# Twelve VectorE additions of the first MoE layer made into ScalarE copies with accumulating DMAs

## The chip, the cores and the metric

The kernel runs on one core of a Trainium2 chip. The metric is the device time of one execution in microseconds, lower is better. A run gives several executions; the median is compared.

## The reference, cut to what matters

The kernel fuses three layers: attention with a tanh cap, a first MoE layer (w1, w2) and a second one (w3, w4) with a softmax-like gate and a layer norm. The change lies in the second product of the first MoE layer.

```python
def _moe_ref(x, w_in, w_out):       # x 1792 x 768, w_in 768 x 2048, w_out 2048 x 768
    h = x @ w_in
    g = h - np.tanh(h)
    return (g @ w_out).astype(np.float32)
...
x = attention(q, k, v, cap)         # (1792, 768)
x = _moe_ref(x, moe_w_in, moe_w_out)
return _moe2_ref(x, moe2_w_in, moe2_w_out, moe2_g_ln)
```

## The kernel before, in words

The work is done in two halves of 896 tokens (`hb` 0 and 1), each in three stages: attention, `moe1`, `moe2`. Every matrix product is made of three matmuls on high and low parts (`wh`, `wl` of a weight, `xh`, `xl` or `gh`, `gl` of an activation).

**Weights.** They come as pairs of 32-bit words. In the first half a unit of weights (512 KB) is loaded into a staging tile `st` (L104, three buffers, SyncE's DMA queue, called SP below), three VectorE instructions put the words together in `f` (L109, L110, L111; three buffers), ScalarE writes the high part (L117) and VectorE the low part (L118). SP then saves the result to HBM (L134, `d<-w`), where the second half reads it, so that only the first half converts. In what follows, a conversion is one such L109, L110, L111 and L118. The conversion runs many units ahead of the matmuls, through a ring of 14 weight tiles.

**moe1.** The hidden dimension is cut into four chunks (`NCHUNK`). `up(c)` makes four blocks `hp` of 128 hidden rows by 896 tokens in PSUM (pool "a", two buffers; L416, L418), and `nonlinear` (L442 to L460) turns each into `gh` and `gl`: ScalarE reads `hp` twice (L444 into `u`, L446 into `t`), VectorE twice (L450 and L453), and after L453 the PSUM buffer is free. Tiles `u` have two buffers. `down(c)` makes six output blocks `op` (L472, L474; pool "b", two buffers), 24 matmuls each, and adds each to its accumulator `acc[d]` in SBUF: for chunk 0 ScalarE copies (L479), for later chunks VectorE adds in two instructions of 448 columns (L481); the last chunk also splits the sum into `yh` and `yl` (L483, L484). TensorE runs up(1), down(0), up(2), down(1), up(3), down(2), down(3).

**Order of the work.** In `moe1` the order of each engine's queue is set by the framework's scheduler, which goes by its own estimates; once the program is built each engine runs its list strictly in order. GpSimd's queue (POOL) carries in this stage only the DMAs that wait for the next attention.

Of the kernel before, what the change touches and what calls it, by code (L numbers as in the profile page):

```python
# [9 lines left out]
F32 = mybir.dt.float32  # L10
# [4 lines left out]
ALU = mybir.AluOpType  # L15
# [14 lines left out]
def fused_kernel(ctx, tc, qk_in, v, cap, w1, w2, w3, w4, gln, out):  # L30
    nc = tc.nc
    B, H, S, D = 4, 12, 448, 64
    DM = H * D
    P = 128
# [14 lines left out]
    NCHUNK = w2.shape[0] // NK  # L49
# [11 lines left out]
    @contextmanager  # L61
    def banks(name, *tags):
        with ExitStack() as st:
            for tag, n in tags:
                psum[tag] = st.enter_context(tc.tile_pool(name=name + tag, bufs=n, space=PSUM, reuse_waits="tile"))
            yield

    def pst(name, tag="b"):
        return psum[tag].tile([P, 2, 512], F32, tag=tag, name=name)
# [130 lines left out]
    def load_w1(c, half):  # L200
        ts = []
        for i in range(NK // 2):
            ts += cols(unit(f"1_{c}_{half}_{i}", w1u[(c * 2 + half) * (NK // 2) + i], 2), 2)
        return ts

    def load_w2(c, d):
        return cols(unit(f"2_{c}_{d}", w2u[c * NK + d], CH // P), CH // P)
# [193 lines left out]
        while pending:  # L401
            keep()

    def moe1(mp, xh, xl, yh, yl):
        acc = [mp.tile([P, HT], F32, tag=f"acc{d}", name=f"acc{d}", bufs=1) for d in range(NK)]
        gs = {}
        place.update(pool=(mp, WX1), at=-1)

        def up_mms(hp, wt, m, k0, k1, gg=(0, 1)):
            ms = slice(m * P, (m + 1) * P)  # L410
            for kk in range(k0, k1):
                wh, wl = wt[kk]
                xs = [(xh[kk][:, g * S:(g + 1) * S], xl[kk][:, g * S:(g + 1) * S]) for g in range(2)]
                for i in range(2):
                    for g in gg:
                        nc.tensor.matmul(hp[:, g, :S], wh[:, ms], xs[g][i], start=(kk == 0 and i == 0), stop=False)  # L416
                for g in gg:
                    nc.tensor.matmul(hp[:, g, :S], wl[:, ms], xs[g][0], start=False, stop=(kk == NK - 1))  # L418

        def first():  # L420

            gs[0] = []
            wts = [load_w1(0, 0), load_w1(0, 1)]
            hps = [pst("hp", "ab"[half]) for half in range(2) for _ in range(2)]
            for g, k0, k1 in ((0, 0, NK), (1, 0, 3), (1, 3, 4), (1, 4, 5), (1, 5, 6)):
                for m in range(3):
                    up_mms(hps[m], wts[m // 2], m % 2, k0, k1, (g,))
                    if k1 == NK and g == 1:
                        nonlinear(0, hps[m])
            up_mms(hps[3], wts[1], 1, 0, NK)  # L430
            nonlinear(0, hps[3])

        def up(c, half):
            gs.setdefault(c, [])
            wt = load_w1(c, half)
            for m in range(2):
                hp = pst("hp", "a")
                up_mms(hp, wt, m, 0, NK)
                nonlinear(c, hp)

        def nonlinear(c, hp):
            h = hp[:, :, :S]  # L442
            u = mp.tile([P, 2, S], F32, tag="u", name="u")
            nc.scalar.activation(u, h, AF.Square)  # L444
            t = mp.tile([P, 2, S], F32, tag="t", name="t")
            nc.scalar.activation(t, h, AF.Tanh)  # L446
            mk = mp.tile([P, 2, S], U8, tag="mk", name="mk")
            nc.scalar.activation(mk, t, AF.Square, scale=TS)
            gf = mp.tile([P, 2, S], F32, tag="gf", name="gf")
            nc.vector.scalar_tensor_tensor(gf, u, C2, h, ALU.mult, ALU.mult)  # L450
            w = mp.tile([P, 2, S], F32, tag="w", name="w", bufs=1)
            nc.scalar.activation(w, u, AF.Square, bias=gat)
            nc.vector.tensor_tensor(t, h, t, ALU.subtract)  # L453
            nc.vector.scalar_tensor_tensor(gf, w, GB, gf, ALU.add, ALU.mult)
            nc.vector.copy_predicated(gf, mk, t)
            gh = mp.tile([P, 2, S], F32R, tag="gh", name="gh", bufs=6)
            gl = mp.tile([P, 2, S], F32R, tag="gl", name="gl", bufs=6)
            nc.scalar.copy(gh, gf)  # L458
            nc.vector.tensor_tensor(gl, gf, gh.bitcast(F32), ALU.subtract)
            gs[c].append((gh, gl))  # L460

        def down(c):
            for d in range(NK):
                wt = load_w2(c, d)
                op = pst("op")
                nm = CH // P
                for m in range(nm):
                    gg = gs[c][m]
                    wh, wl = wt[m]
                    for i in range(2):  # L470
                        for g in range(2):
                            nc.tensor.matmul(op[:, g, :S], wh, gg[i][:, g], start=(m == 0 and i == 0), stop=False)  # L472
                    for g in range(2):
                        nc.tensor.matmul(op[:, g, :S], wl, gg[0][:, g], start=False, stop=(m == nm - 1))  # L474
                for g in range(2):
                    cs = slice(g * S, (g + 1) * S)
                    a = acc[d][:, cs]
                    if c == 0:
                        nc.scalar.copy(a, op[:, g, :S])  # L479
                    else:  # L480
                        nc.vector.tensor_tensor(a, op[:, g, :S], a, ALU.add)  # L481
                    if c == NCHUNK - 1:
                        nc.scalar.copy(yh[d][:, cs], a)  # L483
                        nc.vector.tensor_tensor(yl[d][:, cs], a, yh[d][:, cs].bitcast(F32), ALU.subtract)  # L484

        first()
        for c in range(NCHUNK):
            if c + 1 < NCHUNK:
                up(c + 1, 0)
                up(c + 1, 1)  # L490
            down(c)
# [136 lines left out]
    @contextmanager  # L628
    def pools(name, *groups):
        with ExitStack() as st:  # L630
            yield Region([(g, st.enter_context(tc.tile_pool(name=f"{name}{i}", bufs=2, reuse_waits="tile")))
                          for i, g in enumerate(groups)])

    def xtiles():
        return ([xp.tile([P, HT], F32R, tag="xh", name="xh") for _ in range(NK)],
                [xp.tile([P, HT], F32R, tag="xl", name="xl") for _ in range(NK)])

    rest = None
    for hb in range(2):
        xh, xl = xtiles()  # L640
        with pools(f"a{hb}", ("t",), ("kqh", "kql"), ("ou",), ("rb", "rs", "su"), None) as ap, banks(f"pa{hb}", ("s", 1), ("o", 2)):
            with tc.manual_schedule(engines=ORD):
                attention(ap, hb, xh, xl, rest)
        yh, yl = xtiles()
        if hb == 0:
            nc.sync.dma_start(glt, gln.rearrange("(c p) -> p c", p=P))
        with pools(f"m{hb}", ("gh", "gl"), ("wx",), ("acc",), None) as mp, banks(f"pm{hb}", ("a", 2), ("b", 2)):
            moe1(mp, xh, xl, yh, yl)
        with pools(f"n{hb}", ("h2g",), ("wx",), ("lh0", "ll0"), None, ("e",), ("lh1", "ll1")) as mp, banks(f"pn{hb}", ("a", 2), ("b", 2)):
            rest = moe2(mp, hb, yh, yl)  # L650

# [62 lines left out]
```

## Time and profile before

| | |
|---|---|
| three runs | 931.48, 932.25, 938.44 us; median 932.25 |
| profiled execution | 931.82 us, of which the profile's span is 930.0 |
| mean granted TensorE clock | 0.991 |
| instructions | 12258 |

The profile holds for each engine every instruction with start and duration, and for a wait what ended it. Times in it are microseconds from the start of the span. The span is one execution, so a sum made from it is compared with 931.82 first and then set beside the median.

### The profile page before, as it was taken

The page shows a single profiled execution, that of the slowest core. Times are in us where ns is not written, and L with a number is a line of the kernel's source. Part 1 is how long each engine was busy: PE and PEld are TensorE (multiplying, and loading weights), DVE is VectorE, ACT ScalarE, POOL GpSimd, SP SyncE. Part 2 cuts the span into 40 slices and gives each one's busy share as a digit, 9 for nine tenths or more (in the row PEclk, how much of TensorE's full clock was granted, in tenths as well). Part 3 has the DMA queues.
Part 4 walks back from the last instruction along what each step waited for, and adds up shares of the span by engine and source line. Part 5 has one row for each costly group of instructions (what it writes and reads, how often), then busy time and mean ns, then how long its engine had stood idle before and what let it go on. Part 6 is the DMA issues. An engine that isn't in the chain of part 4 may idle for free.

```text
span 930.0 us, 12258 instructions
## 1 busy us (share of the span) xinstructions
PE 909.5 (98%) x4864; PEld 736.2 (79%) x4864; DVE 583.8 (63%) x918; ACT 418.1 (45%) x459; POOL 46.8 (5%) x88
## 2 busy tenths in 40 slices
PE   6999998999999999999999999999999999999998
PEld 4444487999989998888874446899999999888887
DVE  5677589999989994688423443793363644305851
ACT  6999328546335222352258882573340511212321
POOL 2211000000000000001022110000000000000000
PEclk9999989999999999999999999999999999999999
DMA  7564383398685875531154641524333232221311
GB/s 246 160 210 131 112 334 128 104 329 290 215 270 194 276 272 205 173 146 78 53 201 167 204 137 38 171 79 133 105 113 113 86 124 87 91 83 53 134 48 51
DMA packets 49500, 142.92 MB, mean 154 GB/s; under 512 B 13540, under 2 KB 16612, under 8 KB 49444
## 3 DMA queue, kind: packets, MB, share of 16 engines
q1 hardware_dynamic: 42260, 112.95, 35.4%
q0 software_dynamic: 7040, 29.20, 9.3%
q8 instruction: 38, 0.62, 0.3%
q14 instruction: 18, 0.15, 0.1%
q10 hardware_dynamic: 144, 0.00, 0.0%
HBM read 98.64 MB, written 43.33 MB: 153 GB/s over the span
## 4 chain that ended last, share of the span: by engine, by line
PE 74%; DVE 12%; DMA 9%; issue 2%; ACT 2%; SPq 0%; DVEq 0%; ACTq 0%
PE op L472 13%; PE hp L416 9%; PE op L474 6%; PE o L302 6%; PE s L270 5%; PE hp L418 4%; PE hp L223 4%; PE hp L224 4%; PE hp L225 4%; PE so L319 3%; DMA rs<-su 2%; PE oab L572 2%; PE oab L576 2%; PE oab L573 2%; DMA rb<-rd 2%
## 5 line engine op out<-in xcount | busy, mean ns | idle before, releaser
L416 PE MATMUL hp<-xh,w 128*128 128x448 f32 x384 | 118.2, 374 | 9.2 <-DVE t L453 4.8
L416 PE MATMUL hp<-xl,w 128*128 128x448 f32 x384 | 117.3, 372 | 0.4 <-DVE xl L361 0.4
L418 PE MATMUL hp<-xh,w 128*128 128x448 f32 x384 | 116.0, 369 | 0.0
L474 PE MATMUL op<-gh,w 128*128 128x448 f32 x336 | 95.7, 365 | 0.0
L472 PE MATMUL op<-gl,w 128*128 128x448 f32 x336 | 95.4, 365 | 0.0
L472 PE MATMUL op<-gh,w 128*128 128x448 f32 x336 | 95.4, 365 | 0.0
L416 PEld LDWEIGHTS hp<-xh,w 128*128 128x128 f32 x384 | 73.4, 192 | 18.8 <-issue 7.0
L416 PEld LDWEIGHTS hp<-xl,w 128*128 128x128 f32 x384 | 73.8, 192 | 8.8 <-issue 1.4
L418 PEld LDWEIGHTS hp<-xh,w 128*128 128x128 f32 x384 | 73.1, 190 | 5.9
L302 PE MATMUL o<-t,vf 128*64 128x448 f32 x384 | 77.5, 545 | 0.0
L294 ACT ACTIVATE t<-t,shift,capt 128x3136 f32<-128x3136 f32 (+2 forms) x26 | 72.7, 2806 | 0.7
L481 DVE TENSOR_TENSOR acc<-op,acc 128x448 f32<-128x448 f32 x72 | 41.8, 617 | 44.6 <-PE op L474 44.5
L472 PEld LDWEIGHTS op<-gh,w 128*128 128x128 f32 x336 | 63.1, 188 | 5.0
L472 PEld LDWEIGHTS op<-gl,w 128*128 128x128 f32 x336 | 63.1, 188 | 5.0
L474 PEld LDWEIGHTS op<-gh,w 128*128 128x128 f32 x336 | 63.1, 188 | 5.0
L223 PE MATMUL hp<-w,xh 128*128 128x512 f32 x168 | 65.5, 390 | 0.0
L225 PE MATMUL hp<-w,xl 128*128 128x512 f32 x168 | 65.4, 389 | 0.0
L224 PE MATMUL hp<-w,xh 128*128 128x512 f32 x168 | 65.4, 389 | 0.0
L458 ACT CAST gh<-gf 128x896 fp32r<-128x896 f32 x32 | 30.2, 944 | 72.5 <-PE op L474 47.4
L444 ACT ACTIVATE u<-hp 128x896 f32<-128x896 f32 x32 | 29.5, 920 | 71.2 <-PE hp L418 71.0
L117 ACT CAST w<-f 128x512 fp32r<-128x512 f32 x44 | 27.3, 622 | 71.9 <-DVE f L111 52.2
L302 PEld LDWEIGHTS o<-t,vf 128*64 128x64 f32 x384 | 25.4, 136 | 40.8 <-issue 40.2
(146 smaller groups left out, 1681.0 us busy)
## 6 DMA issues: line engine op xcount, KB each, us to landing
d<-w SPq DMA_DIRECT2D x69, 512.0 KB
w<-d SPq DMA_DIRECT2D x56, 512.0 KB
st<-in_moe_w_out_dram SPq DMA_DIRECT2D x35, 512.0 KB
st<-in_moe_w_in_dram SPq DMA_DIRECT2D x25, 512.0 KB
kq<-in_qk_dram POOLq DMA_DIRECT2D x21, 480.0 KB, 5.0
w<-d POOLq DMA_DIRECT2D x13, 512.0 KB, 6.0
st<-in_moe_w_in_dram POOLq DMA_DIRECT2D x11, 512.0 KB, 6.0
vf<-in_v_dram POOLq DMA_DIRECT2D x22, 256.0 KB, 5.0
```

The lines of the kernel that those rows point to most:

```text
L223: nc.tensor.matmul(ps, sh, mh, start=first, stop=False)
L224: nc.tensor.matmul(ps, sh, ml, start=False, stop=False)
L225: nc.tensor.matmul(ps, sl_, mh, start=False, stop=last)
L270: nc.tensor.matmul(s[:, 2 * r + hh, :S], st[rows, cs], mv[rows, KW:], start=first, stop=last)
L294: nc.scalar.activation(t[:, sl], t[:, sl], AF.Exp, bias=shift, scale=capt)
L302: nc.tensor.matmul(o[cs, :S], vf[:, r, cs], t[:, 6 if r == 3 else 2 * r + hh], start=(r == 0), stop=(r == 3))
L416: nc.tensor.matmul(hp[:, g, :S], wh[:, ms], xs[g][i], start=(kk == 0 and i == 0), stop=False)
L418: nc.tensor.matmul(hp[:, g, :S], wl[:, ms], xs[g][0], start=False, stop=(kk == NK - 1))
L458: nc.scalar.copy(gh, gf)
L472: nc.tensor.matmul(op[:, g, :S], wh, gg[i][:, g], start=(m == 0 and i == 0), stop=False)
L474: nc.tensor.matmul(op[:, g, :S], wl, gg[0][:, g], start=False, stop=(m == nm - 1))
L481: nc.vector.tensor_tensor(a, op[:, g, :S], a, ALU.add)
```

## The change

In the first half only (`hb == 0`), for the two middle chunks (c = 1 and 2), the finished block `op` is copied out whole by ScalarE (896 columns, from PSUM) into a tile `part`, and a DMA issued by GpSimd adds `part` to `acc[d]` (`accum_op=ALU.add`). `part` takes its buffers from the tag `u`, the two buffers that the nonlinearity's squares use. The two VectorE additions for that block are left out. The second half is unchanged.

```diff
-    def moe1(mp, xh, xl, yh, yl):
+    def moe1(mp, hb, xh, xl, yh, yl):
...
+                if hb == 0 and 0 < c < NCHUNK - 1:
+                    part = mp.tile([P, 2, S], F32, tag="u", name="part")
+                    nc.scalar.copy(part, op[:, :, :S])
+                    nc.gpsimd.dma_start(acc[d], part.rearrange("p g s -> p (g s)"), accum_op=ALU.add)
+                    continue
                 for g in range(2):
...
-            moe1(mp, xh, xl, yh, yl)
+            moe1(mp, hb, xh, xl, yh, yl)
```

The scheduler makes new lists for VectorE and ScalarE from it. VectorE's list before, at the end of down(1)'s stretch and up to the first nonlinearity of up(3) (L450 on `hp_2329`); `f` and `st` numbers name single conversions:

```order
L109 TENSOR_SCALAR f_2851<-st_2849 128x512
L118 TENSOR_TENSOR wx_2768<-f_2771,wx_2768 128x512
L118 TENSOR_TENSOR w_2806<-f_2809,w_2806 128x512
L110 SCALAR_TENSOR_TENSOR f_2851<-st_2849,f_2851 128x512
L111 SCALAR_TENSOR_TENSOR f_2851<-st_2849,f_2851 128x512
L109 TENSOR_SCALAR f_2893<-st_2891 128x512
L110 SCALAR_TENSOR_TENSOR f_2893<-st_2891,f_2893 128x512
L111 SCALAR_TENSOR_TENSOR f_2893<-st_2891,f_2893 128x512
L450 SCALAR_TENSOR_TENSOR gf_2372<-u_2366,hp_2329 128x896
L109 TENSOR_SCALAR f_2935<-st_2933 128x512
L454 SCALAR_TENSOR_TENSOR gf_2372<-w_2374,gf_2372 128x896
L453 TENSOR_TENSOR t_2368<-hp_2329,t_2368 128x896
```

From the last VectorE instruction that is the same in both lists (L454 of up(2)'s fourth block) to this L450 the list holds 10 conversions (their L109, L110 and L111), 10 L118, 12 additions L481, one L455 and two L459. The same place in the changed program (the block is called `hp_2335` there):

```order
L110 SCALAR_TENSOR_TENSOR f_2905<-st_2903,f_2905 128x512
L118 TENSOR_TENSOR w_2860<-f_2863,w_2860 128x512
L111 SCALAR_TENSOR_TENSOR f_2905<-st_2903,f_2905 128x512
L109 TENSOR_SCALAR f_2947<-st_2945 128x512
L110 SCALAR_TENSOR_TENSOR f_2947<-st_2945,f_2947 128x512
L111 SCALAR_TENSOR_TENSOR f_2947<-st_2945,f_2947 128x512
L109 TENSOR_SCALAR f_2989<-st_2987 128x512
L110 SCALAR_TENSOR_TENSOR f_2989<-st_2987,f_2989 128x512
L111 SCALAR_TENSOR_TENSOR f_2989<-st_2987,f_2989 128x512
L450 SCALAR_TENSOR_TENSOR gf_2378<-u_2372,hp_2335 128x896
L454 SCALAR_TENSOR_TENSOR gf_2378<-w_2380,gf_2378 128x896
L453 TENSOR_TENSOR t_2374<-hp_2335,t_2374 128x896
```

The same stretch now holds 12 conversions, 11 L118, no addition, one L455 and two L459: two more conversions stand ahead of L450. ScalarE's list before, over the same stretch, from the casts of down(1) to `u` of up(3)'s first block:

```order
L117 CAST w_2692<-f_2695 128x512
L458 CAST gh_2010<-gf_2003 128x896
L458 CAST gh_2064<-gf_2057 128x896
L117 CAST w_2730<-f_2733 128x512
L117 CAST wx_2768<-f_2771 128x512
L117 CAST w_2806<-f_2809 128x512
L444 ACTIVATE u_2366<-hp_2329 128x896
```

And in the changed program, from the copy of down(1)'s fourth block on (the first three copies stand ahead, with casts between them):

```order
L477 COPY part_2221<-op_2196 128x896
L117 CAST w_2740<-f_2743 128x512
L117 CAST wx_2779<-f_2782 128x512
L477 COPY part_2260<-op_2235 128x896
L458 CAST gh_2010<-gf_2003 128x896
L117 CAST w_2818<-f_2821 128x512
L458 CAST gh_2064<-gf_2057 128x896
L477 COPY part_2299<-op_2274 128x896
L117 CAST w_2860<-f_2863 128x512
L444 ACTIVATE u_2372<-hp_2335 128x896
```

The copies now stand among the casts and ahead of `u`; `u_2372` takes the buffer of `part_2260`. The lists of TensorE are the same, SP's loads and saves keep their sequence but for a few neighbours, and GpSimd's list gains 12 DMAs ahead of the loads of the next attention.

## Rows read from the trace of the kernel before

**Rows 1.** The page: span, and busy time, share and instructions by engine.
```profile
span 930.0 us, 12258 instructions
PE 909.5 (98%) x4864; PEld 736.2 (79%) x4864; DVE 583.8 (63%) x918; ACT 418.1 (45%) x459; POOL 46.8 (5%) x88
```

**Rows 2.** Slices of 10 us: busy time of engines, TensorE's clock, DMA share, GB/s.
```profile
260.00:270.00 10.00, 10.00 (x51) 9.26 (x51) 10.00 (x18) 3.28 (x5) 0.00 (x0) 1.00 0.85 277
270.00:280.00 10.00, 8.01 (x39) 7.14 (x38) 7.08 (x12) 4.62 (x6) 0.00 (x0) 0.98 0.79 258
280.00:290.00 10.00, 10.00 (x44) 9.13 (x44) 10.00 (x15) 6.11 (x8) 0.00 (x0) 0.85 0.63 253
```

**Rows 3.** Waits of PE, 100 to 410 us: us in total, times, longest.
```profile
PE hp L416 <- DVE t L453: 4.8, 2, 2.8
PE hp L416 <- DVE xh L360: 3.9, 1, 3.9
PE hp L416 <- DVE xl L361: 0.2, 1, 0.2
```

**Rows 4.** PE's timeline: start, us, instruction, in brackets idle time before it.
```profile
277.05 0.57 PE L418 MATMUL hp<-xh,w 128*128 128x448 f32 x2
279.61 1.08 PE L416 MATMUL hp<-xh,w 128*128 128x448 f32 x2 [1.99 <-DVE t L453]
```

**Rows 5.** DVE's timeline, down(1) to up(3)'s first block.
```profile
240.69 0.60 DVE L481 TENSOR_TENSOR acc<-op,acc 128x448 f32<-128x448 f32 x1
241.22 1.16 DVE L455 COPY_PREDICATED gf<-mk,t 128x896 f32<-128x896 uint8 x1
...
261.73 2.08 DVE L459 TENSOR_TENSOR gl<-gf,gh 128x896 fp32r<-128x896 f32 x2
263.74 0.68 DVE L118 TENSOR_TENSOR w<-f,w 128x512 fp32r<-128x512 f32 x1
264.34 1.15 DVE L481 TENSOR_TENSOR acc<-op,acc 128x448 f32<-128x448 f32 x2
265.40 0.75 DVE L109 TENSOR_SCALAR f<-st 128x512 uint32<-128x512 uint32 x2
266.07 1.28 DVE L110 SCALAR_TENSOR_TENSOR f<-st,f 128x512 uint32<-128x512 uint32 x2
267.28 1.28 DVE L111 SCALAR_TENSOR_TENSOR f<-st,f 128x512 uint32<-128x512 uint32 x2
...
274.25 0.43 DVE L109 TENSOR_SCALAR f<-st 128x512 uint32<-128x512 uint32 x1 [2.81 <-DMA st<-in_moe_w_out_dram]
...
276.04 1.08 DVE L450 SCALAR_TENSOR_TENSOR gf<-u,hp 128x896 f32<-128x896 f32 x1
```

**Rows 6.** The chain that ended last, 240 to 290 us: its two DMA pieces.
```profile
252.40 5.50 DMA st<-in_moe_w_out_dram
...
267.99 6.24 DMA st<-in_moe_w_out_dram
```

**Rows 7.** ACT's timeline around the place.
```profile
238.79 0.62 ACT L117 CAST w<-f 128x512 fp32r<-128x512 f32 x1 [0.91 <-DVE f L111]
...
270.36 0.92 ACT L444 ACTIVATE u<-hp 128x896 f32<-128x896 f32 x1 [1.14 <-PE hp L418]
```

**Rows 8.** The page's DMA parts: queues (share of 16 engines), issues (KB each, us to landing).
```profile
q1 hardware_dynamic: 42260, 112.95, 35.4%
...
kq<-in_qk_dram POOLq DMA_DIRECT2D x21, 480.0 KB, 5.0
w<-d POOLq DMA_DIRECT2D x13, 512.0 KB, 6.0
```

**Rows 9.** DVE's timeline, down(2) into down(3).
```profile
301.57 0.62 DVE L481 TENSOR_TENSOR acc<-op,acc 128x448 f32<-128x448 f32 x1
...
323.11 2.09 DVE L459 TENSOR_TENSOR gl<-gf,gh 128x896 fp32r<-128x896 f32 x2
...
330.20 1.15 DVE L481 TENSOR_TENSOR acc<-op,acc 128x448 f32<-128x448 f32 x2
```

## The prediction, made before the changed kernel was run

> **What bounds the kernel now.** I read the page first. TensorE is busy 909.5 of 930.0 us [rows 1], so whatever the other engines gain can at most fill TensorE's holes. Next come the waits of PE over both MoE stages of the first half: three lines, 8.9 us in all, and only one of them, the wait for VectorE's L453, can belong to the changed stretch (the L36x lines are attention's) [rows 3]. It comes twice; the longer, 2.8 us, is at about 157 us, before down(1) has begun, out of the change's reach. The other is 1.99 us at 279.61 [rows 4].
>
> So the reachable time is one hole. The 10 us slices show what it costs: TensorE works 8.01 of 10 us in the slice at 270 and then runs at a mean granted clock of 0.85 in the slice at 280, where it was 1.00 before [rows 2]; part of that slice is on the lower of the two levels, 1.2 instead of 2.4 GHz, and 15% of 10 us is 1.5 us more. The hole is worth 2.0 + 1.5 = 3.5 us, and with 0.2 from the clock of 0.98 in the slice at 270, 3.7 us.
>
> Why is it there? VectorE's timeline tells [rows 5]. L450, the first VectorE step on up(3)'s first block, begins at 276.04, though its input `u` was ready at 270.36 + 0.92 = 271.28 [rows 7]. In front of it stand two conversions, and the second waited 2.81 us for its staging load. The chain that ended last runs through just that load: 6.24 us from the L111 that freed its buffer to its L109, and 5.50 us for an earlier one [rows 6]. VectorE is full (10.00 of 10 us in the slices at 260 and 280) except where it waits (7.08 at 270) [rows 2]; but what ends last is a weight load that stands, by list order, ahead of work that TensorE needs.
>
> **The change part by part.**
>
> *Removed:* 24 additions on VectorE. A pair takes 264.34 to 265.40 = 1.06 us from start to start [rows 5], so six pairs per chunk free 6.4 us, 12.7 us over both chunks. None of this is on the end's path by itself; it counts only through L450.
>
> *Added on ScalarE:* 12 copies of 128x896 from PSUM. The nearest row is L444, same shape and source, 0.92 us [rows 7]; I take 0.95. ScalarE is busy 3.3 to 6.1 us of 10 there [rows 2], so 5.7 us per 29 us of down are hidden under TensorE, as long as no copy waits; behind a waiting copy stand casts and `u` (a rival, below).
>
> *Added on GpSimd:* 12 DMA issues. Behind them on its queue stand only loads that wait for the next attention: no cost.
>
> *Added on the DMA engines:* 12 transfers of 448 KB from SBUF to SBUF. The trace shows no accumulating DMA. From the queue shares, q1 moves 112.95 MB in 35.4% of 930 us, 343 GB/s with all 16 engines [rows 8]; one plain pass of 458,752 bytes is then 1.34 us of all engines. The low end is nothing that anyone feels (the engines idle 15 to 37% of these slices [rows 2]); the high end is two passes, since the destination must be read too, 2.7 us, with every transfer delaying the load beside it. One transfer comes per output block, some 4.8 us apart (the additions of the first and the sixth block began at 240.69 and 264.34 [rows 5]), so a load in flight for about 5.9 us meets 1.2 of them: +0 to +3.3 us per load. I take +0.8, half of the single pass, nearest to the plain rows.
>
> The Trainium skill ("DMA: Bandwidth & Descriptors", section on the anatomy of one DMA on the SWDGE path) fits such a DMA as 2.0 us plus bytes over 436e3 per us, 3.05 us for ours as an estimate. The trace has 5.0 and 6.0 us to landing for 480 and 512 KB on the same queue [rows 8], and is followed; by the page's figure a load would be slowed by at most 1.2 x 1.05 us and the sum would stay within 1 us of mine.
>
> *Moved:* the list in front of L450. Before: 10 conversions; now 12. Steps from the timeline [rows 5]: L109 0.34 (half of 265.40 to 266.07), L110 0.60 (half of 266.07 to 267.28), L111 0.60 (as long as L110), L118 0.60 (263.74 to 264.34), a pair of L459 2.01 (261.73 to 263.74); L455 is 1.16 long and, as the others do, overlaps the next by some 0.1: 1.06. Both lists part at 240.69. Without any wait the old list needs 10 x 1.54 + 10 x 0.60 + 12 x 0.53 + 1.06 + 2.01 = 30.8 us, to 271.5; 276.04 is what the waits for loads made of it. The new one needs 12 x 1.54 + 11 x 0.60 + 1.06 + 2.01 = 28.2 us, to 268.9. So by work alone L450 could run as soon as `u` is there, 271.3.
>
> But the loads bind more. There are three staging buffers, so the load of a conversion is issued when the third before it has done L111. Call the twelve a to l and the time from that L111 to the L109 it serves λ (5.5 and 6.24 us by rows 6). a ends L111 at 240.69 + 0.60 + 1.06 + 0.60 + 0.67 + 1.21 + 0.60 = 245.4. Then d waits λ and takes 2.14 with the L118 inside it; g waits λ, and f's L111 stands behind g's L109 (0.34 + 0.60); i waits λ and takes 1.54; l waits λ and takes 1.54; then L450. Sum: L450 = 251.6 + 4λ. TensorE restarts 3.23 us after L450: now it is 279.61 - 276.04 = 3.57, and the L109 that stands between L450 and L454 (0.34) is gone from there. It is free for it at 277.62 [rows 4].
>
> With λ = 5.67 the hole is just gone; with 6.2 it is as now; with 5.9, the mean of both rows, it is 0.9. With 5.9 + 0.8 = 6.7, L450 stands at 278.4, TensorE restarts at 281.6 instead of 279.6: +2.0 us. The slower clock after the hole is paid already; for a hole twice as long I add 0.3. At the high end, λ = 9.2, the restart is at 291.6, +12.0.
>
> *Down(2):* here the list has the two L459 for down(3) behind eight conversions. By the same steps, from 301.57 [rows 9], they begin at 309.7 + 2λ, 323.1 with λ = 6.7, where they began at 323.11 before [rows 9] without a wait of TensorE. No cost up to λ of about 8.8.
>
> Sum: 931.82 + 2.3 = 934.1 against the profiled execution; this stands 0.43 below the median of the runs, so 934.5 on their scale.
>
> **The rivals.**
>
> *The hole closes (faster).* If the freed 6.4 us let the loads start early and they land in 5.5 us or less, L450 is at 273.6 and TensorE never waits: 932.25 - 3.7 = 928.5. For it: the row of 5.50, and DMA engines idle for part of the stretch. Against it: engines busy at 0.85 and 0.79 just there [rows 2], and six more transfers.
>
> *ScalarE held by the two buffers (slower).* The third copy of a chunk must wait until the first one's DMA has landed, and so on; `u` of up(3) takes the buffer of the fifth. If a DMA takes L from issue to landing, copy one ends at 240.4 (238.79 + 0.62 for the cast ahead of it [rows 7], + 0.95) and `u` cannot begin before 240.4 + 3L + 2 x 0.95. That passes 270.36 from L = 9.4. With L = 14, `u` is at 284.3, L450 at 285.2, TensorE at 288.5: +8.9. In down(2) the same chain frees the fifth block's PSUM buffer at 301.5 + 2L + 1.9 = 331.4, while TensorE wants it at about 325 (the first addition of down(3) runs at 330.20, one block later [rows 9]): +6.4. Together 932.25 + 15.3, about 947.5. For it: an unmeasured kind of DMA into busy engines; against it: 5.0 and 6.0 us for plain ones [rows 8]. The Trainium skill ("SBUF — State Buffer", section on its two separate sides) has a rule that would lengthen L: a DMA issued by GpSimd cannot get its descriptors written while VectorE holds the port they share in its fast modes, and VectorE is full here. In rows 8 the same queue's DMAs landed in 5 to 6 us beside a VectorE that was less full (63% over the span [rows 1]).
>
> *Hidden anyway.* λ stays at 5.9 to 6.2 and the hole as it is: within 1 us of 932.25. It is the lower edge of my own case.
>
> **How the numbers follow.** 1% is 9.3 us, about what a measurement of this kernel can tell from no change. My case, λ between 6.2 and 8.5 and so 0 to +9 us: 0.55. The hole shrinks or closes, 0 to -3.7: 0.27. ScalarE held: 0.12. λ above 8.5 without that: 0.06. The gain is capped at 3.7 us, 0.4%, so faster by over 1% gets 0.01. Slower by over 1% is the last two, 0.18, a little more for the upper edge of my case: 0.19. The remaining 0.80 is within 1%. The range runs from the closed hole, 928.5, to λ = 9.2, 932.25 + 12.3, about 944.5; the rival at 947.5 is left out.
>
> **What would show it right or wrong.** In the profile after: the additions gone from VectorE in 240 to 326 us and the conversions packed together; an idle time of VectorE before L109, ended by a staging load, several times between 245 and 276; PE's wait for L453 in up(3), 2 to 6 us; the load pieces in the chain at 6 to 8 us. I am wrong if that wait is gone, if PE waits for ScalarE or for L477, or if `part` or `u` wait for a DMA for several microseconds.

## The result and the profile after

The changed kernel takes 941.28 us (median of 10 runs, 937.69 to 947.97), the kernel before, run beside it, 932.76 us (10 runs, 931.35 to 941.90). The ratio is 1.008, 95% interval 1.0054 to 1.0105: slower by 5 to 10 us. The execution that was profiled took 945.01 us, 3.7 above the median; its span is 943.2 us.

The page of the kernel after, span and busy time by engine, as [rows 1], and its DMA view, as [rows 8]: two queues (packets, MB, share of 16 engines) and the new transfer (KB each, us from issue to landing).

```profile
span 943.2 us, 12303 instructions
PE 917.4 (97%) x4864; PEld 739.3 (78%) x4864; DVE 573.6 (61%) x894; ACT 427.7 (45%) x471; POOL 57.7 (6%) x100
```

```profile
q1 hardware_dynamic: 42260, 112.95, 34.4%
q0 software_dynamic: 8768, 34.71, 12.3%
...
acc<-part POOLq DMA_DIRECT2D x12, 448.0 KB, 8.9
```

The work did move as meant: VectorE has 24 instructions and 10 us less, ScalarE 12 instructions and 10 us more. But no engine that was freed sets the end. The largest part of the loss that shows is one hole of TensorE. Its waits from 100 to 420 us in the kernel after, as [rows 3]:

```profile
PE hp L416 <- DVE t L453: 9.0, 2, 6.5
```

and TensorE's timeline at the longer one, which is the place of [rows 4], before up(3)'s third block:

```profile
280.54 0.57 PE L418 MATMUL hp<-xh,w 128*128 128x448 f32 x2
287.60 1.09 PE L416 MATMUL hp<-xh,w 128*128 128x448 f32 x2 [6.48 <-DVE t L453]
```

The hole of 1.99 us has become 6.48. Why L453 was late stands in VectorE's timeline, the stretch of [rows 5]. The last of the conversions ahead of L450, each waiting in brackets for its load:

```profile
275.11 0.43 DVE L109 TENSOR_SCALAR f<-st 128x512 uint32<-128x512 uint32 x1 [1.58 <-DMA st<-in_moe_w_out_dram]
...
279.92 0.43 DVE L109 TENSOR_SCALAR f<-st 128x512 uint32<-128x512 uint32 x1 [2.45 <-DMA st<-in_moe_w_out_dram]
...
282.38 0.43 DVE L109 TENSOR_SCALAR f<-st 128x512 uint32<-128x512 uint32 x1 [0.58 <-DMA st<-in_moe_w_out_dram]
...
284.18 1.08 DVE L450 SCALAR_TENSOR_TENSOR gf<-u,hp 128x896 f32<-128x896 f32 x1
```

ScalarE had written `u` long before (275.50 + 0.92 = 276.4, first row below). That row also shows the two shared buffers at work: `u` waited 1.32 us for an accumulating transfer, and the copies of both chunks 6.5 us (second row, from the waits of ACT between 235 and 375 us). Neither ends last.

```profile
275.50 0.92 ACT L444 ACTIVATE u<-hp 128x896 f32<-128x896 f32 x1 [1.32 <-DMA acc<-part]
```

```profile
ACT part L477 <- DMA acc<-part: 6.5, 2, 5.0
```

The chain that ended last has three load pieces in that stretch, where there were two [rows 6], of 5.50 and 6.24 us:

```profile
247.11 6.12 DMA st<-in_moe_w_out_dram
...
257.91 9.30 DMA st<-in_moe_w_out_dram
...
273.56 8.80 DMA st<-in_moe_w_out_dram
```

And the 16 DMA engines have no room left there. Before and after over down(1) and the first half of up(3); the columns are those of [rows 2], the last two DMA share and GB/s:

```profile
240.00:280.00 40.00, 38.01 (x187) 34.95 (x186) 36.12 (x62) 11.37 (x16) 0.00 (x0) 0.99 0.80 264
```

```profile
240.00:280.00 40.00, 40.00 (x195) 36.33 (x195) 28.81 (x48) 17.24 (x25) 5.48 (x6) 1.00 1.00 305
```

The share went from 0.80 to 1.00 (1.03 to 1.05 in the three slices of 10 us from 250 on; since it passes 1, the times of packets can overlap a little, and 1 is about full and not an exact ceiling), while VectorE went from 36 to 29 busy microseconds of 40: it stands idle for loads. The GB/s rose by 41 only: the accumulating transfers take much engine time for the bytes that they are booked with.

### The profile page after: what moved, and what is told of

Its sections match the earlier page's. It is cut to its first block, busy times and chain, and to the rows that moved or that the text cites. A ratio compares the mean times of both kernels' runs of the same rounds, so it can differ in the third digit from the quotient of the medians.

```text
span 943.2 us, 12303 instructions
## 1 busy us (share of the span) xinstructions
PE 917.4 (97%) x4864; PEld 739.3 (78%) x4864; DVE 573.6 (61%) x894; ACT 427.7 (45%) x471; POOL 57.7 (6%) x100
## 3 DMA queue, kind: packets, MB, share of 16 engines
q0 software_dynamic: 8768, 34.71, 12.3%
## 4 chain that ended last, share of the span: by engine, by line
PE 70%; DMA 13%; DVE 10%; issue 3%; SPq 2%; ACT 2%; DVEq 0%
PE op L472 13%; PE hp L416 9%; PE op L474 7%; DMA rs<-su 5%; PE hp L418 5%; PE hp L225 4%; PE hp L223 4%; PE hp L224 4%; PE o L302 4%; PE s L270 4%; DMA st<-in_moe_w_out_dram 3%; PE oab L577 2%; PE oab L581 2%; PE oab L578 2%; DMA rb<-rd 2%
## 5 line engine op out<-in xcount | busy, mean ns | idle before, releaser
L416 PE MATMUL hp<-xh,w 128*128 128x448 f32 x384 | 119.3, 377 | 14.9 <-DVE t L453 9.0
L418 PE MATMUL hp<-xh,w 128*128 128x448 f32 x384 | 117.6, 373 | 0.0
L458 ACT CAST gh<-gf 128x896 fp32r<-128x896 f32 x32 | 30.1, 944 | 71.7 <-PE op L474 45.1
L450 DVE SCALAR_TENSOR_TENSOR gf<-u,hp 128x896 f32<-128x896 f32 x32 | 34.8, 1086 | 36.3 <-ACT t L446 30.9
L486 DVE TENSOR_TENSOR acc<-op,acc 128x448 f32<-128x448 f32 x48 | 27.9, 619 | 46.4 <-PE op L474 46.4
```

## The experiments

Three theories stood against each other at first: that the transfers slow the staging loads, and the conversions ahead of L450 in VectorE's list carry the lateness to TensorE; that ScalarE is held by the two buffers that copies and `u` share; and that it is not the transfers at all but the new list or the copies.

Two lengths are read from each trace by the first matmuls of the stages: up(3), which has no hole where it takes 29.2 us, and down(2) with down(3), 58.3 us without a hole. (At the slower matmul pace told of at the end these are 29.7 and 59.5.) The ratios are to the kernel before run beside each.

| run | ratio, 95% interval | up(3) | down(2), down(3) |
|---|---|---|---|
| before | | 32.9 | 58.4 |
| after | 1.008, 1.0054 to 1.0105 | 38.3 | 59.5 |
| e1, copies, no transfer | 0.9973, 0.9938 to 1.0008 | 29.7 | 59.5 |
| e2, plain transfer | 0.9973, 0.9945 to 1.0001 | 33.1 | 59.5 |
| e3, chunk 1 only | 1.0054, 1.0014 to 1.0093 | 38.5 | 59.5 |
| e4, chunk 2 only | 1.0007, 0.9977 to 1.0037 | 32.2 | 63.9 |
| e5, after with late list | 1.008, 1.0049 to 1.011 | 29.8 | 64.2 |
| e6, after with six buffers | 1.0081, 1.005 to 1.0112 | hole in down(1) | 61.3 |
| e7, before with late list | 0.9979, 0.9955 to 1.0003 | 29.7 | 59.5 |
| e8, after with four staging buffers | 1.0012, 0.999 to 1.0035 | 29.7 | 59.5 |
| e9, two plain transfers | 1.0102, 1.0069 to 1.0135 | 38.0 | 58.3 |
| e10, before with four staging buffers | 1.0051, 1.0025 to 1.0077 | 29.8 | 59.5 |
| e11, after with a lent buffer | 1.0099, 1.0065 to 1.0132 | 40.1 | 64.6 |
| e12, before with a lent buffer | 0.994, 0.9909 to 0.997 | 29.2 | 58.3 |

**e1 and e2: the transfer taken out, and made plain.**

```diff
-                    nc.gpsimd.dma_start(acc[d], part.rearrange("p g s -> p (g s)"), accum_op=ALU.add)
+                    pass
```

```diff
-                    nc.gpsimd.dma_start(acc[d], part.rearrange("p g s -> p (g s)"), accum_op=ALU.add)
+                    nc.gpsimd.dma_start(acc[d], part.rearrange("p g s -> p (g s)"))
```

Expected of e1: 

> The twelve copies stay, their DMAs are left out (so the middle chunks are missing from the sums); every engine's list is otherwise that of the changed kernel. Theory A (the DMAs make the staging loads late that stand ahead of L450): the hole before up(3)'s third block falls from 6.5 us to 1 to 2 us and the time to 931 to 934 us. Theory B (ScalarE waits for the two buffers of u until the DMAs have landed): the same, since nothing is waited for. Theory C (the new list alone, with two more conversions ahead of L450): the hole stays at 5 us or more and the time at 938 us or more.

Expected of e2: 

> The same DMAs without the addition, so each overwrites the accumulator; every list is the same. Theory A: a plain transfer takes half the DMA engines' time of an accumulating one (1.3 us instead of 2.5), so the loads are late by half as much: hole 2 to 5 us, 934 to 938 us. Theory B: landing falls from 8.9 us to 5 to 6 us, below the point at which the buffers bind, so the hole is gone: 929 to 932 us. If the addition itself costs nothing: as the changed kernel, about 941 us.

Both take 0.9973 of the kernel before (934.59 and 934.35 us against 935.39), with the lists and the copies of the change. So the 8.5 us are not the list, nor the copies, nor a transfer of 448 KB as such; they come with `accum_op`. e1 has no wait of TensorE at all from 235 to 375 us. e2 still has the hole before up(3)'s third block, within theory A's 2 to 5 us and larger than before; theory B had it gone. Waits of PE, 235 to 375 us, in e2:

```profile
PE hp L416 <- DVE t L453: 3.4, 1, 3.4
```

What one transfer takes follows from the queue's share in the DMA views of e1, e2 and after (above):

```profile
q0 software_dynamic: 7040, 29.20, 9.3%
```

```profile
q0 software_dynamic: 8000, 34.71, 10.9%
...
acc<-part POOLq DMA_DIRECT2D x12, 448.0 KB, 6.5
```

Without transfers q0 has 0.093 x 932.7 = 86.7 us of all 16 engines; with twelve plain ones 0.109 x 932.9 = 101.7, 1.25 us each; with twelve accumulating ones 0.123 x 943.2 = 116.0, 2.44 us each (the shares are rounded to 0.1%, which is 0.08 us per transfer). An accumulating transfer takes the engines about twice as long as a plain one, and lands after 8.9 instead of 6.5 us. The Trainium skill ("DMA: Bandwidth & Descriptors", section "Rules for kernel authors") says that an accumulate reads its destination and writes it later; that fits a price of two passes. No run here shows the second read itself. The counts in the three lines also give an accumulating transfer 144 packets ((8768 - 7040) / 12) where the plain one has 80, for the same bytes; whether the double time comes from a second pass or from more and smaller packets was not tried. e9 tests whether the double time is enough to make the loss.

**e3 and e4: one chunk alone.**

```diff
-                if hb == 0 and 0 < c < NCHUNK - 1:
+                if hb == 0 and c == 1:
```

(in e4 `c == 2`).

Expected of e3: 

> Only chunk 1 is copied and added by DMA; chunk 2 is added by VectorE as before. If the loss is the one hole in up(3) (theories A, B and C alike): hole about 6 us, time 938 to 941 us, all of the change's loss. If the loss is spread over both chunks: about 936 to 937 us.

Expected of e4: 

> Only chunk 2 is copied and added by DMA. If the loss is the one hole in up(3): hole about 2 us as before, time 931 to 934 us, no loss. If the loss is spread over both chunks: about 936 to 937 us.

Chunk 1's six transfers alone make the hole (6.8 us) and a loss of some 5 us (ratio 1.0054; the interval goes from 1 to 9 us, so it can't be told whether that is all of the 8.5). With chunk 2's alone it stays at 2.2 us and the ratio's interval takes in 1. In e4's profile, though, there is a new hole after down(2), at the place that the prediction had looked at: TensorE waits for the L459 of down(3), behind conversions in the list.

```profile
PE op L472 <- DVE gl L459: 3.9, 1, 3.9
```

**e5: the list repaired.** The last chunk's down weights from the second slice on are put behind the L453 of up(3)'s first block; four conversions fewer stand ahead of L450.

```diff
...
+                if first_half[0] and c == NCHUNK - 1 and d >= 1:
+                    with tc.issue_after(place["mark", c, 0].ins):
+                        wt = load_w2(c, d)
...
```

Expected: 

> The changed kernel with one edit: in the first half, the load and conversion of the last chunk's down weights from the second slice on (load_w2(3, d), d >= 1) are put in the list behind the last activation step (L453) of up(3)'s first block. The accumulating transfers stay. Theory A (the transfers make the staging loads late, and the conversions that stand ahead of L450 in VectorE's list carry the lateness to TensorE): with four conversions fewer ahead of that step, TensorE's wait for L453 in up(3) falls from 6.5 us to under 2, and the time to 933 to 936, ratio to before 0.998 to 1.002, with the accumulating transfers as long as they were (8.9 us to landing). Theory B (ScalarE held by the two buffers that the copies and L444's u share): the wait stays near 6.5 us, 940 to 942. Theory C (the engines' share taken by the transfers costs time by itself, wherever the list has its conversions): the lateness shows up one stage later, in down(2) or down(3), at 938 to 942.

Measured 941.61 us against 933.73, ratio 1.008: nothing gained, though the hole before up(3)'s third block is gone. TensorE waits one stage later instead, in down(2), which takes 64.2 us instead of 59.5 (the stages of this execution are at the slower pace). Waits of PE, 235 to 375 us, in e5 (its L459, L460, L482 and L491 are L458, L459, L477 and L486 of the kernel after):

```profile
PE op L477 <- DVE acc L491: 2.2, 1, 2.2
PE op L477 <- ACT part L482: 1.0, 1, 1.0
PE op L477 <- DVE gl L460: 0.8, 1, 0.8
PE op L477 <- ACT gh L459: 0.7, 1, 0.7
```

So theory A has the path of the changed kernel right, but its remedy falls: theory C of this run held, in which the engines' time is short wherever the list has its conversions. The waits of the four rows add up to 4.7 us. Whether chunk 1's lateness was carried into down(2), or chunk 2's own six transfers made it there, as they do alone in e4, was not parted.

**e6: six buffers for the copies.**

```diff
-                    part = mp.tile([P, 2, S], F32, tag="u", name="part")
+                    part = mp.tile([P, 2, S], F32, tag=("u", "t", "gf")[d % 3], name="part")
```

Expected: 

> The changed kernel with the part copies' buffers taken in turn from three pairs (tags u, t and gf) in place of one pair, so that a copy waits for a transfer six copies back. Theory A: ScalarE's waits for the transfers (6.5 us for L477 and 1.3 for L444 between 235 and 375 us) go, the hole before up(3)'s third block stays at 5 to 7 us, and the time at 939 to 943, ratio to before 1.006 to 1.010. Theory B: the hole falls to about 2 us and the time to 933 to 936.

Measured 942.57, ratio 1.0081, as A has it. ScalarE no longer waits for a transfer there, and the time is the same. The hole is not where A put it, a miss: TensorE's wait for L453 in up(3) falls to 1.5 us, as B has it, and another hole has come. The new list of ScalarE has casts ahead of the copy, the casts wait for conversions and these for loads, and TensorE waits in down(1) for a PSUM buffer. ACT's timeline, then PE's, in e6:

```profile
254.54 0.62 ACT L117 CAST w<-f 128x512 fp32r<-128x512 f32 x1 [5.58 <-DVE f L111]
256.81 0.62 ACT L117 CAST w<-f 128x512 fp32r<-128x512 f32 x1 [1.65 <-DVE f L111]
257.33 0.90 ACT L477 COPY part<-op 128x896 f32<-128x896 f32 x1
```

```profile
258.28 1.12 PE L472 MATMUL op<-gh,w 128*128 128x448 f32 x2 [4.79 <-ACT part L477]
```

So e6 alone doesn't clear the two buffers. The trace of the kernel after does: `u` was ready 7.8 us before L450 began. And so does e8 (below), where the copies and `u` wait 21.1 us for transfers and TensorE has no hole. Waits of ACT, 235 to 375 us, in e8:

```profile
ACT part L477 <- DMA acc<-part: 16.2, 5, 4.9
ACT u L444 <- DMA acc<-part: 4.9, 1, 4.9
```

**e9: the same traffic without accumulation.** Each accumulating transfer becomes two plain ones.

```diff
-                    nc.gpsimd.dma_start(acc[d], part.rearrange("p g s -> p (g s)"), accum_op=ALU.add)
+                    nc.gpsimd.dma_start(acc[d], part.rearrange("p g s -> p (g s)"))
+                    nc.gpsimd.dma_start(acc[(d + 4) % NK], part.rearrange("p g s -> p (g s)"))
```

Expected: 

> The changed kernel with each accumulating transfer replaced by two plain ones of the same 448 KB: one to the block's own place and one to that of the block four further (mod 6). The additions of the two middle chunks are left out. Theory T (traffic: an accumulating transfer costs what it costs because it takes the 16 engines twice as long): q0's share goes to 12 to 12.6%, the loads' waits are like those of the changed kernel (lateness of L450 in up(3) 4 us or more above the kernel before's, 17 to 19 us after up(3)'s start), and the time is 938 to 942, ratio 1.005 to 1.010. Theory L (what costs is something of the accumulation alone, such as a read that must come back before the write goes out, which two independent transfers don't have): the time stays within 2 us of the single plain transfer's, ratio 0.996 to 1.001, though q0's share is the same.

Measured 944.63 us against 933.93, ratio 1.0102, a little above theory T's range, with the same hole in the same place (L450 18.5 us after up(3)'s start). Queue, and PE's timeline, in e9:

```profile
q0 software_dynamic: 8960, 40.21, 12.1%
```

```profile
288.94 1.08 PE L416 MATMUL hp<-xh,w 128*128 128x448 f32 x2 [6.86 <-DVE t L453]
```

0.121 x 945.2 = 114.4 us in q0, 2.31 us for a pair. Theory T holds: two plain transfers cost the kernel what one accumulating transfer costs, so the engines' double time is enough to explain the loss, and the addition needs no price of its own.

**e7, e8, e10: what loads and buffers can repair.** e7 is e5's edit on the kernel before. e8 and e10 give the loads a fourth staging buffer, and take one from the ring of weights.

```diff
-    WA, WX1, WX2 = 13, 1, 0
+    WA, WX1, WX2 = 13, 0, 0
...
-        st = sp.tile([P, 512, 2], U32, tag="st", name="st", bufs=3)
+        st = sp.tile([P, 512, 2], U32, tag="st", name="st", bufs=4)
...
```

Expected of e7: 

> The kernel before with the edit of the late list alone (load_w2(3, d), d >= 1, of the first half behind L453 of up(3)'s first block); VectorE keeps its 48 additions. If the 2 us hole before up(3)'s third block, and the clock after it, is worth what the prediction says (3.7 us), and the list alone makes it: the hole goes and the time is 928 to 931, ratio 0.995 to 0.998. If other work is late right behind it: 932 to 934, no difference.

Expected of e8: 

> The changed kernel with four staging buffers in place of three (and one ring buffer fewer, 13 for 14). If what costs is the latency of a load (each load is issued only when its buffer is free, so that the last conversion ahead of L450 comes after four latencies in a row): with four buffers it comes after three, some 9 us sooner, the hole closes and the time is 932 to 935, ratio 0.998 to 1.001. If it is the transfer time itself (the 16 engines are at 1.03 to 1.05 of their span from 250 to 280 us, so a fourth buffer only lengthens the queue): the hole stays at 4 to 7 us and the time at 938 to 942. With one ring buffer fewer, weights may come late elsewhere by 0 to 2 us.

Expected of e10: 

> The kernel before with four staging buffers for three and one ring buffer fewer, the control for the changed kernel with four. If the missing ring buffer costs the 4.8 us that TensorE lost between 130 and 170 us in that run's profile, and the fourth staging buffer closes the 2 us hole before up(3)'s third block: 933 to 936, ratio 1.000 to 1.004, and the change itself is then worth between -2 and +2 us once loads have a fourth buffer. If the fourth buffer alone is worth more than the ring buffer: 929 to 932.

e7: 931.76 against 933.73, ratio 0.9979. The 2 us hole is gone; the interval reaches 1.0003, so a gain is likely and not shown. e8: 936.21 against 933.73, ratio 1.0012; no hole of TensorE from 235 to 375 us. e10: 938.04 against 933.93, ratio 1.0051. Both lose some 5 us ahead of up(2) (its first matmul at 166.0 and 165.5 us, for 160.1 before), where the end of attention comes late: PE's waits for L360, 100 to 425 us, in e10, are 6.7 us where they were 3.9 [rows 3], which is 2.8 of the 5.

```profile
PE hp L416 <- DVE xh L360: 6.7, 3, 4.3
```

That loss blurs what e8 seems to say, that a fourth buffer hides the transfers: in e8 TensorE comes to up(3) 6.8 us later than before, which gives the loads that much more time. But e10, which loses as much ahead of up(2) and has no accumulating transfers, is not faster than e8 (the intervals overlap, in separate comparisons): between these two the change costs nothing that can be told. e11 and e12 were made to take the blur away.

**e11 and e12: a fourth buffer in this stage only.** Every fourth load of the stage lands in the ring's extra buffer, which the ring gives up there; attention keeps what it had.

```diff
+        if "loads" in place:
+            place["loads"] += 1
+        if place.get("loads", 0) % 4 == 1:
+            st = place["pool"][0].tile([P, 512, 2], U32, tag="wx", name="sx", bufs=1)
+        else:
+            st = sp.tile([P, 512, 2], U32, tag="st", name="st", bufs=3)
...
-        place.update(pool=(mp, WX1), at=-1)
+        place.update(pool=(mp, WX1 if "2_3_5" in saved else 0), at=-1)
+        if "2_3_5" not in saved:
+            place["loads"] = 0
...
     def moe2(mp, hb, yh, yl):
+        place.pop("loads", None)
```

Expected of e11: 

> The changed kernel with a fourth staging buffer that exists in the first half's first MoE layer only: every fourth weight load of that stage lands in the ring's extra buffer (tag wx), which the ring gives up there; attention before it keeps its three staging buffers and its ring of 13. If four staging buffers remove the lateness and the loss between 130 and 170 us of the other four-buffer kernels came from their buffer in attention: no wait for L453 over 2 us in up(3), and the time 929 to 933, ratio 0.995 to 1.000, which would beat the kernel before. If the transfers' traffic still makes a stage late (the 16 engines at 1.03 to 1.05): 936 to 940.

Expected of e12: 

> The kernel before with the same lent buffer and VectorE's 48 additions kept: the control. If the fourth buffer closes the 2 us hole before up(3)'s third block: 928 to 931, ratio 0.995 to 0.998, and the change on top of it is worth the difference to the other run, expected within 2 us. If the earlier start of the loads in attention was worth more than the buffer: 934 to 938.

e12 beats both kernels: 928.87 us against 934.92, ratio 0.994, interval 0.9909 to 0.997. Waits of PE, 100 to 425 us, in e12 (its L365 is the L360 of before): only attention's is left, and both waits for L453 [rows 3], 4.8 us, are gone.

```profile
PE hp L423 <- DVE xh L365: 4.1, 1, 4.1
```

e11, the change on top of e12, is a clear miss for the theory that a buffer mends it, and above the other theory's range too: 944.33 us, ratio 1.0099, so the change costs 1.6% here, about 15 us. Waits of PE, 235 to 375 us, in e11 (its lines stand seven further on than in the kernel after):

```profile
PE hp L423 <- DVE t L460: 7.9, 1, 7.9
PE op L479 <- DVE gl L466: 3.8, 2, 3.6
```

The DMA shares differ, e12 first, then e11, 245 to 285 us (busy time and count of L114, which is the L109 of before, then granted clock, DMA share, GB/s):

```profile
245.00:285.00 40.00, 3.96 (x10) 1.00 0.78 277
```

```profile
245.00:285.00 40.00, 4.22 (x10) 0.89 1.01 345
```

In e12 TensorE reaches up(3) 5 us sooner than in the kernel before (257.7 for 262.9 us), and 32 conversions have begun by 235 us where there were 35. The engines still have 22% to spare for the rest. With the transfers on top they are full, and L450 comes 10.3 us later than in e12 (277.2 for 266.9 us). Full engines alone don't make the hole, though: e8 has the same share in the same 40 us, and no wait of TensorE.

```profile
245.00:285.00 40.00, 3.81 (x9) 1.00 1.01 315
```

What differs is the lead. Of the conversions that stand ahead of L450, five had not begun when TensorE came to up(3) in e11 (258.0 us) and in the kernel after (266.1 us), and two in e8 (269.7 us); before and e12 have four, with room on the engines. That this lead is what decides is a reading of the traces; no run changes the lead alone.

## Why the prediction was right, and where its size was off

*Direction and place: right.* It named the hole before up(3)'s third block, the path (transfer, load, conversion, L450, L453) and the sign. The ratio's interval gives +5 to +10 us, the medians +8.5, where +2.3 was said: the time lies in the range because the range was wide, from -3.7 to +12.3.

*The hole.* Predicted: TensorE free at 277.62, back at 281.6, a hole of 4.0 us. Measured 6.48: the term of +2.0 was +4.5.

*The step that failed: "I take +0.8, half of the single pass".* The bounds were right, one pass at 1.34 (plain: 1.25 measured) and two at 2.7 (accumulating: 2.44 measured), but I took the value near the lower end because plain transfers were the nearest rows, though I had written that the destination must be read too. The loads on the chain took 6.12, 9.30 and 8.80 us, 8.1 on average, where λ was put at 6.7; the sum had four of them in a row, the chain has three. I also read the engines as idle for 15 to 37% from slices that begin at 260 [rows 2]; the slice before them, in the same stretch, was nearly full:

```profile
250.00:260.00 10.00, 10.00 (x51) 9.27 (x50) 9.04 (x18) 2.22 (x4) 0.00 (x0) 1.00 0.96 312
```

*The form of that step failed too.* A delay per load, as if a transfer met each load by chance, takes no account of engines that are full. Their time could have been summed from the slices: a share of 0.80 from 240 to 280 us (the row of before, above) is 32.0 us of work in 40; six transfers of 2.44 add 14.6, which makes 46.6, or 6.6 us too much. With 1.25 us each it is 39.5, just within (e2 measured 0.98 of the 40). Measured: L450 came 8.1 us later than before (284.18 for 276.04), of which 1.5 are this execution's being later already where the lists part (242.18 for 240.69); 6.6 are left. And the plain transfers of e2 cost no time that shows, though its hole is 3.4 us. So the sum tells apart two cases that the range of λ held together; both prices in it lay within my bounds.

That 6.6 meets 6.6 so exactly is luck, and the sum alone doesn't give TensorE's loss. With the additions gone and no transfer (e1, first line) the share in these 40 us is 0.91 and not 0.80, as the loads come sooner. Over down(2) the same sum, from a share of 0.78 before (second line), is 31.2 + 14.6 = 45.8 us in 40; the kernel after is as full there (third line) and VectorE waits 6.3 us for loads (last line), yet TensorE does not wait.

```profile
240.00:280.00 40.00, 40.00 (x196) 36.32 (x195) 36.68 (x58) 17.55 (x24) 0.00 (x0) 1.00 0.91 322
300.00:340.00 40.00, 40.00 (x199) 37.07 (x198) 39.09 (x69) 9.81 (x17) 0.00 (x0) 1.00 0.78 269
330.00:340.00 10.00, 10.00 (x50) 9.07 (x50) 6.09 (x10) 4.67 (x7) 1.74 (x2) 1.00 1.05 327
DVE f L109 <- DMA st<-in_moe_w_in_dram: 6.3, 3, 3.8
```

*The work in the list.* I put 28.2 us for it, and 9.5 us of waits on top (278.4 - 268.9). From the parting of the lists to L450 it is 284.18 - 242.18 = 42.0 us, and VectorE's waits for these loads, as the waits of DVE from 235 to 375 us give them, are

```profile
DVE f L109 <- DMA st<-in_moe_w_out_dram: 11.4, 6, 3.7
```

all six of them before L450. So the waits were 1.9 us short, and the work, 30.6, was 2.4 short. Two terms were too small, then, and of the 4.3 us by which L450 missed its forecast (284.18 - 1.49 - 278.4) this one has the larger part. A conversion that runs alone takes longer than half of two that run interleaved: in [rows 5] the last one goes from 274.25 to L450 at 276.04, 1.79 us, where I took 1.54.

*The slower clock after the hole: right.* I put 1.7 us, as before, and 0.3 more. The slices after the longer hole (TensorE's clock third from the end):

```profile
280.00:290.00 10.00, 3.52 (x13) 2.85 (x12) 9.18 (x14) 1.46 (x2) 0.00 (x0) 0.74 0.98 395
290.00:300.00 10.00, 10.00 (x46) 9.09 (x45) 9.92 (x15) 6.85 (x10) 0.00 (x0) 0.91 0.48 171
```

By PE's timeline the first six pairs of matmuls after the restart start 0.88, 0.75, 0.75, 0.74, 0.75 and 0.52 us apart (287.60, 288.48, ... 291.99), where it was 0.41 before the hole; that loses 1.9 us. The same count in the kernel before gives 1.6. So it is 1.9 for 2.0, and 0.3 more than before, as said.

```profile
288.48 0.95 PE L416 MATMUL hp<-xl,w 128*128 128x448 f32 x2
```

*Down(2): right for this kernel* (no wait of TensorE there), but not safe: e4, e5 and e11 have it.

*The rivals.* ScalarE held (0.12): the waits exist, the price does not; `u` was ready 7.8 us before L450, and e8 has more of these waits and no hole. A wait of `part` for several microseconds was one of my signs of being wrong; it came (5.0 us) and did not bind. The hole closes (0.27): it does without the transfers, as in e1; e5 closes it too and gains nothing, as TensorE then waits in down(2). Hidden anyway: nearest to that is e2, with plain transfers, whose time is no longer than before, with a hole of 3.4 us.

*What stays open.* Up(3) explains 38.3 - 32.9 = 5.4 us of profile against profile: 4.5 of hole, 0.3 of clock, 0.6 of matmul pace (below). Without the pace, which e1 has too, with no transfer at all, that is 4.8, about where the ratio's interval begins (5.0 us); the rest of the medians' 8.5 us, nearly half, has no hole of its own in the one execution that was profiled, and no run was made for it.

## What to carry to other kernels

Before a DMA is put in place of compute, add its engine time to the DMA share of the slices it will run in, slice by slice. If the sum passes 1, expect the loads beside it to be late. Then ask how far the loads run ahead of the work that needs them: in the kernel after TensorE lost by full engines in up(3) and not in down(2). A new list (e5) and a fourth buffer for the one stage (e11) did not give the time back; in e8, with four buffers throughout and TensorE 6.8 us later, no hole showed. Count an accumulating transfer as two plain ones (2.44 against 1.25 us here). And look at who fills the holes first: here the engine with the full list was not short of time but of loads, and a fourth staging buffer for that one stage (e12) gave 0.6%, about 6 us, more than the change could have given at its best (3.7 us by the prediction).

## What was not expected of the hardware

TensorE has two paces at the full granted clock. The matmuls of 448 columns start 202.7 ns apart, on average, in some stretches of a trace and 206.7 in others, 2.0% slower, with a granted clock of 1.00 in both. The kernel after has the slow pace from about 140 to 360 us and the fast one in its second half; 50 us of each:

```profile
180.00:230.00 50.00, 50.00 (x244) 45.44 (x243) 47.13 (x72) 26.23 (x41) 0.00 (x0) 1.00 0.89 307
660.00:710.00 50.00, 50.00 (x248) 46.39 (x247) 22.85 (x22) 20.66 (x26) 0.00 (x0) 1.00 0.34 106
```

244 recorded matmuls and 45.44 us of weight loading in the one, 248 and 46.39 in the other. In e3, whose program differs only in chunk 2's copies, it is the other way round:

```profile
180.00:230.00 50.00, 50.00 (x248) 46.34 (x247) 47.28 (x74) 26.74 (x40) 0.00 (x0) 1.00 0.88 308
660.00:710.00 50.00, 50.00 (x243) 45.41 (x243) 23.93 (x24) 19.69 (x24) 0.00 (x0) 1.00 0.31 108
```

In the four traces that were gone through for it (after, e1, e3, e12) the pace nearly always changes beside a stop of TensorE, in either sense; what sets it was not tried. Over 100 us it is worth 2 us, so over both halves' MoE stages (some 500 us) up to 10 as an estimate, which is as much as the runs of one kernel spread (931.35 to 941.90 for the kernel before); whether it makes that spread is not shown. Two profiles are compared by stages of the same pace, or not at all.
